# Issuing the broadcast load of the feed-forward scales ahead of the k loads in a fused attention and feed-forward kernel

## The chip, the cores and the metric

The kernel runs on one core of a Trainium2 chip. The core has TensorE (PE in the profile, with its weight loads as PEld), VectorE (DVE), ScalarE (ACT), GpSimd (POOL) and SyncE (SP), which here only issues DMAs. The metric is the device time of one launch in microseconds; lower is better. The kernel before took 1551.76 us in the median of three runs (1550.88, 1551.76 and 1554.2).

## What is computed

```python
def reference(A_x, A_wqkv, A_wo, B_x, B_w_gate, B_w_up, B_w_down):
    x = A_x                                   # 1 x 2048 x 576
    xn = _layernorm(x, axis=-1)
    s = _A_ref(xn, A_wqkv, A_wo)              # attention: 32 heads of 18, window of 256, softmax, then wo
    g = _silu(_B_ref(xn, B_w_gate, B_w_up, B_w_down))
    return x + s * g
...
    def _B_ref(x, w_gate, w_up, w_down):      # 576 -> 4608 -> 576, bilinear
        g = jnp.einsum("bsd,df->bsf", x, w_gate)
        u = jnp.einsum("bsd,df->bsf", x, w_up)
        h = g * u
        return jnp.einsum("bsf,fd->bsd", h, w_down)
```

Inputs and output are float32. The kernel multiplies in float16 with each operand split into a high and a low part, so weights are scaled by powers of two before they are split.

## The kernel before

After a head (layer norm, projection of q, k and v) the kernel runs in 72 slots. A slot does two things side by side. Its feed-forward half multiplies 512 tokens with a quarter of a group of weights: the 4608 hidden columns are cut into 18 groups of 256, numbered 0 to 17, so a group takes four slots. Its attention half, in 64 of the slots, does one pair of heads for one block of 512 queries (step `s`): scores on PE (`score_pairs`, L997), a masked maximum on DVE (`score`, L1006), the exponential and a cast to float16 on ACT (`probs` L1013, `probs_hi` L1018), the low part on POOL (`turn_probs`, L1027), a transposing DMA of both parts (L1030, tile `pt`), and the product with v on PE (`weigh`, L1039). The four query blocks of a step, i = 0 to 3, go through this chain one behind the other; the text calls their casts, low parts and transposing loads cast0 to cast3, low0 to low3 and pt0 to pt3. The tile `pp`, which casts and low parts write and the transposing loads read, has two buffers, so cast3 can start only when pt1 has been read out.

The order of the work on each engine is written out by hand. Every piece of work is put down with a slot and a time in it (`at(slot, t, f, ...)`, a slot is T = 18.65 long), the list is sorted by these times, and the instructions are issued in that order. The times say only who comes before whom; what waits for what is settled by semaphores. Every engine, SP's queue of DMAs included, goes through its own instructions in order, so that an instruction that waits holds up all that are behind it on that engine. The first 248 entries of the list are then put in another order from a table; the entries named below lie behind these.

The scales of group g are made four slots ahead. ACT squares and sums the raw weights into `am` (`ffn_amax`, L532). `ffn_spread_out` adds two halves on POOL (L536) and stores the 128 partial sums to DRAM (SP, L157, tile `sd_f`). `ffn_spread_in` reads them back, all to every partition (SP, L161, tile `spread`, 192 KB). `ffn_scale` takes the maximum over them on DVE (L544) and makes the scales by five small DVE instructions (`root_power`, L146 to L151) and three on POOL (L546 to L548).

```python
spread_in:  t = pool.tile([128, 128, n], F32, name="spread", bufs=1)
            nc.sync.dma_start(t, SD[key].partition_broadcast(128))
...
W = {..., "plo": [2.85, 5.07, 12.24, 14.56], ..., "scale": 14.98, ..., "so": 20.77, "si": 26.88, ...,
     "ld": {"k": 4.98, "q": 9.2, "v": 1.72, ...}}
at(b - 3, W["so"], ffn_spread_out, g)       # b = 4 * g
at(b - 3, W["si"], ffn_spread_in, g)
at(b - 2, W["scale"], ffn_scale, g)
```

In slot b - 2 the store then stands at 20.77 - 18.65 = 2.12 and the load at 26.88 - 18.65 = 8.23. With the times of the other DMAs of that slot, SP's queue holds in order: the store of the sums, pt0, the four loads of k for the next step (`load_k`, L968 and L969, tile `ks`), pt1, the load of the scales, the four loads of q (`load_q`, L976 and L977, tile `qs`), pt2, pt3, the load of v (L984).

PE's side of the same slot: the products of the feed-forward part are at L398, the down projection at L1133 (results in PSUM banks `dn` and `s`), and DVE adds these to the result at L1145. Banks `s` are shared: the scores of L997 lie in them until DVE's L1006 has read them, and one piece of L1133 in the slot takes over such a bank.

Of the kernel before, what the change touches and what calls it, by code (L numbers as in the profile page):

```python
# [20 lines left out]
def kernel(  # L21
# [810 lines left out]
    for half, l in ONE.items():  # L832
        for i, m in enumerate(l):
            b = R[2 * half] + 5.0 - (0 if half else 8.0 - 4.0 * i)
# [23 lines left out]
    for p in range(4):  # L858
        b = W0["qb"][p]
# [44 lines left out]
    b = R[6]  # L904
# [174 lines left out]
    def at(slot, t, f, *a):  # L1079
        todo.append((slot * T + t, len(todo), f, a))  # L1080

    first_slot = 1
    for s in range(NSTEP):
        b = first_slot + s
# [67 lines left out]
    for g in range(NG):  # L1152
        b = 4 * g
        if g > 0:
            for kind, t, u in ((1, W["ld"]["raw1"], 0.1), (2, W["ld"]["raw2"], 0.1), (0, W["ld"]["raw0"], W["raw0"] - W["ld"]["raw0"])):
                for part in range(2):
                    at(b - 3, t + u * part, ffn_raw, g, kind, part)
            for n in range(6):
                at(b - 3, W["amax"][n], ffn_amax, g, (1, 1, 2, 2, 0, 0)[n], n % 2)
            at(b - 3, W["so"], ffn_spread_out, g)  # L1160
            at(b - 3, W["si"], ffn_spread_in, g)
            at(b - 2, W["scale"], ffn_scale, g)
        for k in range(2):
            if g + k > 0:
                c = b if k else b - 2
                at(c, W["sum%d" % k][0], ffn_ratio, g, k)
                at(c, W["sum%d" % k][1], ffn_sums, g, k, 0)
                at(c, W["sum%d" % k][2], ffn_sums, g, k, 1)
                for what in range(4):
                    c = b + k if k and what == 0 else b + k - 1  # L1170
                    at(c, W["whi"][what], w_hi, g, k, what)
                    at(c, W["wlo"][what], w_lo, g, k, what)
        for k in range(2):
            for f, t in ((dn_hi, "dhi"), (dn_lo, "dlo"), (dn_low, "dlow")):
                at(max(0, b + k - 1), W[t], f, g, k)
# [174 lines left out]
    b = NSLOT - 4  # L1350
# [146 lines left out]
```

## Time and profile before

| What | Value |
|---|---|
| median of three runs | 1551.76 us (1550.88 to 1554.2) |
| the profiled execution, its own time | 1554.34 us |
| its span from first to last instruction | 1552.6 us |
| PE busy | 1532.6 us, 99% |
| DVE busy | 1293.8 us, 83% |
| ACT busy | 1047.6 us, 67% |
| POOL busy | 894.5 us, 58% |
| granted PE clock | 1.0 |

A row of a timeline holds the start in us, the duration, the engine, the line, the operation, what it writes and reads, the shape, the number of instructions merged, and in brackets how long the engine sat idle before it and what ended that. SP's rows are the issue of a DMA, not its transfer. A row of the waits holds the waiting engine and line, what it waited for, the sum in us, the number of times and the longest. PE's matmuls are pipelined and their ends are modelled, so a matmul's start is the better guide: between two slots without a stall, the same matmul comes back after 18.53 to 18.54 us.

### The profile page before, as it was taken

The numbers are of one execution on the slowest core, as the hardware profiler recorded it, in microseconds if no ns is written. First come the engines' busy times: TensorE is split into PE (matmuls) and PEld (weight loads), VectorE is DVE, ScalarE is ACT, GpSimd is POOL, SyncE is SP. The second block draws the span as 40 slices with busy tenths as digits, with TensorE's granted clock in tenths as the row PEclk, the third lists the DMA queues.
The fourth block names the chain that finished last, engine by engine and source line by source line (L and its number), as shares of the span: only waits on it lengthen the run. The fifth ranks groups of instructions, "written<-read, shape, count | busy, mean of one in ns | idle before, by whom it ended". The sixth has DMA issues, their size and how long they took to land. (4 is left out here: it accounts for less than half of the span.)

```text
span 1552.6 us, 32644 instructions
## 1 busy us (share of the span) xinstructions
PE 1532.6 (99%) x11791; PEld 882.7 (57%) x11791; DVE 1293.8 (83%) x2974; ACT 1047.6 (67%) x2038; POOL 894.5 (58%) x891
## 2 busy tenths in 40 slices
PE   8999999999999999999999999999999999999998
PEld 5554455555555555555555555555555555555576
DVE  7874777878888989898888889898989798957798
ACT  7655777676677777777777776867677777734243
POOL 5753574647465767666665757575757574822330
PEclk9999999999999999999999999999999999999999
DMA  9444556474747676776777675868685858540544
GB/s 269 132 124 166 164 103 137 92 140 86 151 93 152 137 145 140 139 137 131 151 132 146 128 156 112 163 117 158 121 163 106 167 106 168 104 103 4 113 102 152
DMA packets 562881, 206.06 MB, mean 133 GB/s; under 512 B 492320, under 2 KB 543648, under 8 KB 562720
## 3 DMA queue, kind: packets, MB, share of 16 engines
q1 hardware_dynamic: 562720, 203.98, 62.7%
q8 instruction: 92, 1.51, 0.4%
q14 instruction: 69, 0.57, 0.1%
HBM read 76.63 MB, written 23.75 MB: 65 GB/s over the span
## 5 line engine op out<-in xcount | busy, mean ns | idle before, releaser
L1133 PEld LDWEIGHTS <-hh 128*128 128x128 f16 x3456 | 328.3, 98 | 155.9 <-issue 25.5
L1133 PE MATMUL dn<-dnw,hh 128*128 128x288 f16 x1656 | 248.7, 286 | 2.1 <-DVE acc L1145 2.1
L1133 PE MATMUL s<-dnw,hh 128*128 128x288 f16 x1800 | 243.4, 286 | 3.0 <-DVE mx L1006 2.8
L1145 DVE SCALAR_TENSOR_TENSOR acc<-dn,sc,acc 128x288 f32<-128x288 f32 x260 | 133.5, 513 | 106.7 <-PE dn L1133 106.5
L398 PEld LDWEIGHTS <-wg 128*128 128x128 f16 (+1 forms) x1078 | 104.7, 97 | 121.8 <-issue 29.9
L398 PEld LDWEIGHTS <-stage 128*128 128x128 f16 x1124 | 103.8, 97 | 109.8 <-issue 12.9
L398 PE MATMUL pv<-XT,wg 128*128 128x512 f16 x616 | 154.9, 380 | 0.0
L563 POOL TENSOR_TENSOR stage<-stage 128x256 f32<-128x256 f32 (+1 forms) x180 | 146.5, 831 | 5.5
L398 PEld LDWEIGHTS <-ws 128*128 128x128 f16 x1014 | 93.4, 97 | 98.8 <-issue 13.2
L1145 DVE SCALAR_TENSOR_TENSOR acc<-s,sc,acc 128x288 f32<-128x288 f32 x284 | 139.6, 509 | 10.7 <-PE s L1133 10.1
L398 PE MATMUL up<-XT,ws 128*128 128x512 f16 (+1 forms) x532 | 139.7, 380 | 0.0
L398 PE MATMUL up<-XT,stage 128*128 128x512 f16 (+1 forms) x530 | 138.9, 380 | 0.0
L398 PEld LDWEIGHTS <-wu 128*128 128x128 f16 (+1 forms) x790 | 76.0, 97 | 95.9 <-issue 34.6
L398 PE MATMUL up<-TX,ws 128*128 128x512 f16 x456 | 111.1, 379 | 0.0
L398 PE MATMUL up<-TX,wu 128*128 128x512 f16 x450 | 109.4, 379 | 1.0 <-DVE ftb L427 1.0
L398 PE MATMUL up<-XT,wu 128*128 128x512 f16 (+1 forms) x300 | 110.1, 383 | 0.0
L398 PE MATMUL up<-TX,stage 128*128 128x512 f16 x444 | 108.2, 379 | 0.0
L398 PE MATMUL up<-XT,wg 128*128 128x512 f16 x438 | 106.5, 379 | 0.0
L1039 PEld LDWEIGHTS <-pt 128*128 128x128 f16 x2880 | 91.8, 96 | 19.5 <-issue 0.6
L1039 PE MATMUL pv<-vt,pt 128*128 128x37 f16 x2880 | 93.8, 179 | 0.4 <-DMA pt<-pp 0.4
L1011 ACT ACTIVATE mx<-mx 128x2 f32<-128x2 f32 x256 | 50.9, 199 | 47.3 <-DVE mx L1006 45.7
L532 ACT ACTIVATE spread<-stage 128x640 bf16<-128x640 f32 (+1 forms) x108 | 77.1, 714 | 1.7
(1344 smaller groups left out, 3338.7 us busy)
## 6 DMA issues: line engine op xcount, KB each, us to landing
stage<-in_B_w_down_dram SPq DMA_DIRECT2D x36, 288.0 KB
stage<-in_B_w_gate_dram SPq DMA_DIRECT2D x36, 256.0 KB
stage<-in_B_w_up_dram SPq DMA_DIRECT2D x36, 256.0 KB
vt<-v_d SPq DMA_DIRECT2D x48, 111.0 KB
ks<-qk_d SPq DMA_DIRECT2D x96, 54.0 KB
xr<-in_A_x_dram SPq DMA_DIRECT2D x16, 288.0 KB
qs<-qk_d SPq DMA_DIRECT2D x128, 36.0 KB
stage<-in_A_x_dram SPq DMA_DIRECT2D x16, 288.0 KB
```

The source lines that it names most:

```text
L398: nc.tensor.matmul(ps.rearrange("p (m n) -> p m n", n=128), w, b, start=start, stop=stop, skip_group_check=True)
L532: nc.scalar.activation(j, r, AF.Square, accum_out=SC[g, "am"][:, half, kind:kind + 1])
L563: nc.gpsimd.tensor_tensor(s_[:, d:d + 2] if d < 8 else s_[:, 8], x_, y_, op=op)
L1011: nc.scalar.activation(mx[:, 2:4], mx[:, 0:2], AF.Copy, bias=shift)
L1039: nc.tensor.matmul(PVB[s][:, j, i, :VW], pt[:, 2 * nb * j + n], VT[s][:, lo_ + n % nb, j * VW:(j + 1) * VW], start=n == 0, stop=n == 2 * n ...
L1133: nc.tensor.matmul(ps[:, :HALF], a, b, start=n == 0, stop=n == len(l) - 1)
L1145: nc.vector.scalar_tensor_tensor(d, ps[:, :HALF], SC[g][:, 9:10], d, op0=OP.mult, op1=OP.add)
```

## The change

```diff
@@ -1158,7 +1158,7 @@
             for n in range(6):
                 at(b - 3, W["amax"][n], ffn_amax, g, (1, 1, 2, 2, 0, 0)[n], n % 2)
             at(b - 3, W["so"], ffn_spread_out, g)
-            at(b - 3, W["si"], ffn_spread_in, g)
+            at(b - 3, W["si"] - (3.5 if g > 1 else 0), ffn_spread_in, g)
             at(b - 2, W["scale"], ffn_scale, g)
```

For groups 2 to 17 the load of the scales is put down at 4.73 in slot b - 2 in place of 8.23. In the sorted list nothing else changes its place. On SP's queue the load of the scales moves from behind pt1 to ahead of the four k loads and pt1: store of the sums, pt0, load of the scales, four loads of k, pt1, four loads of q, pt2, pt3. It is one DMA per group. In the slot of group 17 there are no attention steps any more, and the load passes no other DMA.

## The prediction

> **What bounds the kernel now.** I read the page first, then the waits, and then the timelines of single slots, engine by engine.
>
> ```profile
> span 1552.6 us, 32644 instructions
> ...
> PE 1532.6 (99%) x11791; PEld 882.7 (57%) x11791; DVE 1293.8 (83%) x2974; ACT 1047.6 (67%) x2038; POOL 894.5 (58%) x891
> ...
> PE s L1133 <- DVE mx L1006: 2.8, 7, 0.8
> PE s L997 <- DMA qs<-qk_d: 0.6, 2, 0.3
> ...
> DVE sc L544 <- DMA spread<-sd_f: 5.5, 6, 2.1
> ...
> 149.48 0.67 DVE L544 TENSOR_REDUCE sc<-spread 128x3 f32<-128x384 f32 x1 [2.13 <-DMA spread<-sd_f]
> ...
> ACT hh L1113 <- DVE ftd L1105: 79.3, 17, 8.6
> ```
>
> PE is the bound, so only time in which PE stands still moves the result. Its longest wait by name is that of a down projection (L1133) for a bank `s` that DVE's L1006 has yet to read; the seven I looked up lie in slots in which DVE also makes a group's scales. DVE's own wait there for the load of the scales is 5.5 us in six, of which 2.13 belong to group 0, which the change does not touch: 3.4 us in five groups. It looks as if that load were what makes DVE late. The slot of group 13, one of the five, shows otherwise.
>
> ```profile
> 1079.33 0.53 SPq L157 DMA_DIRECT2D sd_f<-am  x1
> ...
> 1082.35 0.96 SPq L968 DMA_DIRECT2D ks<-qk_d  x1
> ...
> 1086.52 1.45 SPq L1030 DMA_TRANSPOSE pt<-pp  x1
> 1088.07 0.79 SPq L161 DMA_DIRECT2D spread<-sd_f  x1
> ...
> 1090.32 0.83 ACT L1018 CAST pp<-sm__15696 128x768 f16<-128x768 f32 x1 [0.84 <-DMA pt<-pp]
> ...
> 1091.23 1.64 POOL L1027 TENSOR_TENSOR pp<-sm__15696,pp 128x768 f16<-128x768 f32 x1 [1.28 <-ACT pp L1018]
> ...
> 1091.61 0.67 DVE L544 TENSOR_REDUCE sc<-spread 128x3 f32<-128x384 f32 x1 [0.32 <-DMA spread<-sd_f]
> 1092.32 0.58 DVE L146 TENSOR_SCALAR sc<-sc 128x3 f32<-128x3 f32 x1
> 1092.93 0.17 DVE L148 TENSOR_SCALAR sc<-sc 128x3 int32<-128x3 int32 x1
> ...
> 1082.56 0.38 PE L398 MATMUL pv<-XT,wg 128*128 128x512 f16 x1
> ...
> 1093.58 0.76 PE L1039 MATMUL pv<-vt,pt 128*128 128x37 f16 x24
> ...
> 1094.90 0.28 PE L1133 MATMUL s<-dnw,hh 128*128 128x288 f16 x1 [0.56 <-DVE mx L1006]
> ...
> 1101.81 0.38 PE L398 MATMUL pv<-XT,wg 128*128 128x512 f16 x1
> ```
>
> L146 works on three elements per partition and takes 0.58 us here. It ends at 1092.90, 30 ns after POOL's low3 (1091.23 + 1.64 = 1092.87). Back from there: low3 starts 0.91 after cast3, and cast3 waited for pt1, which SP had issued 3.80 before it. Forward from there: PE gets its bank 2.00 after L146's end. So PE is held to pt1's issue + 3.80 + 0.91 + 1.64 + 0.03 + 2.00 = pt1's issue + 8.38. The load of the scales, 0.32 late, hid inside that. The control is the slot of group 8, where pt1 is early.
>
> ```profile
> 710.98 0.81 SPq L968 DMA_DIRECT2D ks<-qk_d  x1
> ...
> 712.97 1.44 SPq L1030 DMA_TRANSPOSE pt<-pp  x1
> ...
> 718.05 1.64 POOL L1027 TENSOR_TENSOR pp<-sm__10004,pp 128x768 f16<-128x768 f32 x1 [0.52 <-ACT pp L1018]
> ...
> 719.43 0.28 DVE L146 TENSOR_SCALAR sc<-sc 128x3 f32<-128x3 f32 x1
> ...
> 710.08 0.38 PE L398 MATMUL pv<-XT,wg 128*128 128x512 f16 x1
> ...
> 721.72 0.28 PE L1133 MATMUL s<-dnw,hh 128*128 128x288 f16 x1
> ...
> 728.62 0.38 PE L398 MATMUL pv<-XT,wg 128*128 128x512 f16 x1
> ...
> L146 DVE TENSOR_SCALAR sc<-sc x18: 169/225/650, 150.2 to 1390.0; 128x3 f32<-128x3 f32 x18
> ...
> 204.18 1.01 DVE L148 TENSOR_SCALAR sc<-sc 128x3 int32<-128x3 int32 x1
> ...
> 204.00 1.16 POOL L1027 TENSOR_TENSOR pp<-sm__2110,pp 128x512 f16<-128x512 f32 x1
> ```
>
> Here too L146 ends 20 ns after low3 (719.71 against 719.69), but early enough: PE starts the matmul 11.64 after the slot's first `pv` matmul without a wait, and the slot takes 18.54. In group 13 the same two numbers are 12.34 and 19.25, so the 0.70 is lost whole. Over all 18 groups L146 takes 0.17 at the least and 0.65 at the most. The last pair is an early slot, where a low part starts between two of the small instructions: L148 then takes 1.01 and ends 30 ns after it. POOL's low part and these DVE instructions do not run side by side; DVE waits for the end.
>
> **The change part by part.** Call x the time from the slot's first `pv` matmul to pt1's issue. PE's loss in a slot of scales is x + 8.38 - 11.64 = x - 3.26 where that is positive. In groups 5 to 16 (twelve slots of full width) x is 2.03, 2.94, 2.44, 2.89, 3.47, 2.94, 2.75, 2.42, 3.96, 2.33, 4.11, 4.43; the first and the last:
>
> ```profile
> 484.84 0.50 SPq L157 DMA_DIRECT2D sd_f<-am  x1
> ...
> 487.04 0.83 SPq L968 DMA_DIRECT2D ks<-qk_d  x1
> ...
> 489.06 1.33 SPq L1030 DMA_TRANSPOSE pt<-pp  x1
> ...
> 487.03 1.24 PE L398 MATMUL pv<-XT,wg 128*128 128x512 f16 x5
> ...
> 1312.36 1.43 SPq L1030 DMA_TRANSPOSE pt<-pp  x1
> ...
> 1307.93 0.38 PE L398 MATMUL pv<-XT,wg 128*128 128x512 f16 x1
> 1320.69 0.28 PE L1133 MATMUL s<-dnw,hh 128*128 128x288 f16 x1 [0.60 <-DVE mx L1006]
> ...
> L161 SPq DMA_DIRECT2D spread<-sd_f x18: 333/809/965, 145.3 to 1379.1; - x18
> ...
> 1377.03 0.34 SPq L157 DMA_DIRECT2D sd_f<-am  x1
> 1379.08 0.34 SPq L161 DMA_DIRECT2D spread<-sd_f  x1
> ```
>
> For group 16 the rule gives 1.17, and PE's matmul stands at 12.76, which is 1.12 late. Lost before, group by group: 0.21 (9), 0.70 (13), 1.12 (16), some 0.36 each in groups 7, 10, 11 and 12 where cast3 is late by itself or pt1's issue is slow, and 1.63 in group 15, where load and queries are late as well. That is 5.0 us. The waits by name bear it out: the row's 2.8 in seven, 0.14 more for each by the starts (0.56 idle in group 13 against 0.70 lost) makes 3.8, group 9 adds 0.21, and the waits for q are the rest.
>
> What the change removes: DVE's wait at L544. The load is issued where the first k load was, 5.7 us earlier in group 13 (1082.35 against 1088.07), so it lands long before DVE is there. In group 15 that is worth something; elsewhere low3 takes its place.
>
> What it adds: the load's issue, 0.81 by the median and 0.9 with the gaps around it, now stands ahead of the four k loads and pt1. The k loads have cover, as the q loads, which the same matmuls need, keep their place behind all of this. Pt1 has none. It also has 192 KB more ahead of it in the DMA queue. The queue's share I bound by 0, since pt1 is issued 2.9 after the load, and 0.7, since the load in group 13 lands 3.54 after its issue (1088.07 to 1091.61), 0.64 after that moment. I take 0.3, nearer to 0, because pt1's own issue takes 1.45, in which the queue goes on draining. So pt1 is 1.2 later, between 0.9 and 1.6.
>
> The Trainium skill, page "DMA: Bandwidth & Descriptors", section "Anatomy of one DMA", has the variable part of a transfer as its bytes by 436 GB/s, which makes 0.45 us of 192 KB; by that estimate pt1 would be 1.35 later and the sum about 1 us larger. The measured 3.54 from issue to use is longer than the 2.45 that the same section gives with its fixed 2.0.
>
> What waits for pt1: `weigh`, 3.3 us behind cast3 in group 13 (1093.58), so no loss; cast3 and ACT behind it, where the wait of 79.3 us in 17 (some 4.6 each) follows and covers it; and low3, and through it DVE and PE.
>
> The sum, with x + 1.2 and the spread no longer late. As long as low3 starts before DVE reaches L146 (9.35 after the mark, 719.43 - 710.08), that is up to x = 4.63, the loss is x - 3.26: groups 5 to 8, 10 to 12 and 14 give 0, 0.88, 0.38, 0.83, 0.88, 0.69, 0.36 and 0.27, together 4.3. In groups 9, 13 and 15 (4.67, 5.16, 5.31) low3 starts between the small instructions and the next of them waits for all of its 1.64, as at 204.18: 1.2 each after the spare time, 3.6. In group 16 (5.63) it starts about when they end: 0 or 1.2, so 0.6. After: 8.5. Groups 2 to 4 have narrow, early blocks and group 17 passes nothing: 0. The difference is 8.5 - 5.0 = 3.5 us. With 0.9 in place of 1.2 it is 2.5; with 1.6 it is 5.3.
>
> The profiled execution took 1554.34 (span 1552.6) and would take 1557.8; the median of the three runs, 1551.76, lies 2.6 below it, and I forecast that median: 1555.3.
>
> **The rivals.** Faster: the load of the scales is what holds DVE, and pt1 lands no later because the queue, not the issue, sets its landing. Then the 3.4 us of DVE's wait in five groups go, at most 3.4 for PE: 1548.4. For it speaks that the five groups are also among the losing ones; against it that L146 ends with low3 in groups 13 and 8 alike, and that a rule made from pt1's issue in group 13 gives group 16's matmul to 0.05. It decides if pt1 comes less than about 0.4 later.
>
> No difference: the shift is real but near 0.9, or lost time in one slot lets POOL and SP catch up before the next. Then it is 0 to 3 us: 1553.
>
> Slower by much more: SP, now at the load sooner, stands still until the store of the sums has landed, and k, pt1 and q all wait behind. With nothing else about, SP got to the load 2.05 after the store (group 17). The place that it moves to, the first k load's, is 3.02 after the store in group 13 and 2.20 in group 5, the closest. Were it not to land in time, q would be up to 2 us late and PE would wait at L997, as it does twice now, by about 0.8 in each of twelve groups on top: 1565. It decides where the store needs over 2.2 to 3 us.
>
> The same section of that page puts most of a DMA's fixed 2 us into the receipt from the target memory, heaviest for HBM. By that rule a load right behind its own store would stop the queue; the trace agrees with 2.05 in an idle queue and has no case in a full one.
>
> **How the numbers follow.** This kernel's measurement can tell about 0.2%, 3.1 us, from no change. The mechanism above has 0.70, split at 3.1: 0.47 slower, 0.23 the same. The faster rival has 0.12 (0.09 beyond 3.1), no difference 0.11, the store 0.07. So 0.09 faster, 0.37 the same, 0.54 slower. The likeliest case's own range is 1554.3 to 1557.1, from 2.5 and 5.3. For 8 in 10 I leave out most of the faster rival below and the store above: 1550.3 to 1559.0, which also takes in the spread of the three runs.
>
> **What would show it.** Right: DVE's wait at L544 gone in groups 9 to 16; pt1's issue some 0.9 later against the slot's mark; cast3 waiting for pt1 in nearly every slot of scales, not five; L146 or a small instruction behind it at 0.6 to 1.7 us, ending with low3; PE's wait at L1133 for L1006 grown from 2.8 us in 7 to some 6 in 10 or more. Wrong: L146 at 0.2 to 0.3 throughout and that wait near zero (the faster rival); SP waiting at L161 for `sd_f` (the store). The sum itself would be wrong if low3 falls behind the small instructions in most groups, since then it costs nothing.

## The result

The changed kernel took 1556.26 us in the median of nine executions (1555.41 to 1559.06), the kernel before 1553.29 in nine on the same chip (1550.88 to 1557.4): a ratio of 1.0021, 95% interval 1.0011 to 1.0031. A second comparison gave 1556.93 against 1553.94 and 1.0022 (1.0012 to 1.0032). It is slower by about 3.3 us.

The page of the changed kernel, and below it rows from its waits (engine, line, releaser: us, times, longest):

```profile
span 1554.0 us, 32647 instructions
...
PE 1532.3 (99%) x11791; PEld 882.5 (57%) x11791; DVE 1297.2 (83%) x2974; ACT 1047.8 (67%) x2038; POOL 893.5 (57%) x891
```
```profile
PE s L1133 <- DVE mx L1006: 3.3, 6, 1.2
...
PE s L997 <- DMA qs<-qk_d: 0.5, 1, 0.5
...
DVE sc L544 <- DMA spread<-sd_f: 2.6, 1, 2.6
...
SPq L161 <- DMA sd_f<-am: 9.6, 9, 3.5
```

DVE's wait for the load is gone from every group but group 0, which the change leaves alone: 5.5 us in six have become 2.6 in one. Yet PE's wait for its bank at L1133 has not shrunk (2.8 in seven before). The slot of group 11 shows what took the place of the load:

```profile
935.63 1.99 PE L398 MATMUL pv<-XT,wg 128*128 128x512 f16 x8
...
938.86 1.48 SPq L1030 DMA_TRANSPOSE pt<-pp  x1
...
944.27 0.83 ACT L1018 CAST pp<-sm__13419 128x768 f16<-128x768 f32 x1 [1.48 <-DMA pt<-pp]
944.28 0.67 DVE L544 TENSOR_REDUCE sc<-spread 128x3 f32<-128x384 f32 x1
944.98 0.17 DVE L146 TENSOR_SCALAR sc<-sc 128x3 f32<-128x3 f32 x1
945.18 1.64 POOL L1027 TENSOR_TENSOR pp<-sm__13419,pp 128x768 f16<-128x768 f32 x1 [1.92 <-ACT pp L1018]
945.19 1.66 DVE L148 TENSOR_SCALAR sc<-sc 128x3 int32<-128x3 int32 x1
...
948.64 0.90 PE L1133 MATMUL s<-dnw,hh 128*128 128x288 f16 x6 [1.23 <-DVE mx L1006]
```

The data are there when DVE comes to L544 (no wait in its row). Then low3, which starts 10 ns ahead of L148, holds L148 for its whole length: 1.66 us for three elements per partition. PE's matmul starts 948.64 - 935.63 = 13.01 after the slot's mark in place of 11.62, so 1.39 is lost. In groups 15 and 16, where the kernel before lost 1.66 and 1.14, the same difference is now 0.37 and 0.40. Gains and losses nearly cancel.

The same difference, start of the `s` matmul less the start of the slot's first `pv` matmul less 11.62, can be taken in each of the twelve slots of scales of groups 5 to 16. Their sum is the measure used below for what a kernel loses in these slots, in its profiled execution:

| Kernel | loss in the twelve slots, us | time against the kernel before (95% interval) |
|---|---|---|
| before | 5.26 | 1 |
| only group 17's load moved | 4.90 | 1.0002 (0.9993 to 1.0011) |
| changed: load, k, pt1, q | 4.96 and 4.82 | 1.0021 (1.0011 to 1.0031) and 1.0022 (1.0012 to 1.0032) |
| k, load, pt1, q | 8.65 | 1.0030 (1.0019 to 1.0042) |
| changed, load of 12 KB | 6.01 | 1.0014 (1.0005 to 1.0023) |
| pt1, load, k and q as before | 1.59 | 0.9979 (0.9970 to 0.9988) |
| pt1, k, load, q | 3.79 | 0.9995 (0.9987 to 1.0004) |
| k, q, pt1, load | 13.90 | 1.0089 (1.0075 to 1.0102) |
| before, low3 halved | 1.66 | 0.9987 (0.9977 to 0.9996) |
| changed, low3 halved | 0.32 | 0.9986 (0.9977 to 0.9996) |

The changed kernel's two profiled executions lose no more in these slots than the order before does.

### The profile page after: what moved, and what is told of

Its sections match the earlier page's. It is cut to its first block, busy times and chain, and to the rows that moved or that the text cites. A ratio compares the mean times of both kernels' runs of the same rounds, so it can differ in the third digit from the quotient of the medians.

```text
span 1554.0 us, 32647 instructions
## 1 busy us (share of the span) xinstructions
PE 1532.3 (99%) x11791; PEld 882.5 (57%) x11791; DVE 1297.2 (83%) x2974; ACT 1047.8 (67%) x2038; POOL 893.5 (57%) x891
## 5 line engine op out<-in xcount | busy, mean ns | idle before, releaser
L1133 PEld LDWEIGHTS <-hh 128*128 128x128 f16 x3456 | 328.3, 98 | 156.6 <-issue 26.1
L1133 PE MATMUL dn<-dnw,hh 128*128 128x288 f16 x1656 | 248.7, 286 | 2.1 <-DVE acc L1145 2.1
L1133 PE MATMUL s<-dnw,hh 128*128 128x288 f16 x1800 | 243.4, 286 | 3.6 <-DVE mx L1006 3.3
```

Of the source, the lines that this page charges most:

```text
L1133: nc.tensor.matmul(ps[:, :HALF], a, b, start=n == 0, stop=n == len(l) - 1)
```

## The experiments

The theory was that pt1's place sets low3, low3 holds DVE's small instructions, and these hold PE's bank. The rivals were the load itself, the queue (the store, k and q), and code or scatter with no mechanism in these slots.

**Nothing passed.** Only group 17's load is moved, where the slot has no other DMA to pass:

```diff
-            at(b - 3, W["si"], ffn_spread_in, g)
+            at(b - 3, W["si"] - (3.5 if g > 16 else 0), ffn_spread_in, g)
```

> The load is moved for group 17 alone, where it passes no other DMA, so every queue holds the same DMAs in the same order as before. The theory (pt1 late makes POOL's low part late, which holds up DVE's small instructions and so PE's bank) expects 0 us, and PE's wait at L1133 for L1006 at 2 to 4 us as before. The rival that the difference of the two kernels is scatter of the runs and of the head (the first moved load comes when the changed kernel's profile is already 1.15 us late) expects any value up to 3 us either way here too.

1553.44 against 1553.47. An edit of this line alone is worth nothing. The two executions of the same order also show the noise of a single slot: group 13 lost 0.72 in one and 0.47 in the other, group 9 0.22 and 0.91.

**q ahead of pt1.** This makes pt1 later and leaves the load behind pt1:

```diff
-        at(b - 1, W["ld"]["q"], load_q, s)
+        at(b - 1, 5.03 if s % 4 == 2 and s > 2 else W["ld"]["q"], load_q, s)
```

> The load of the scales stays where it was; the four q loads of the same slots are put ahead of pt1 instead, which puts pt1's issue about 1.8 us later without touching the load or its store. The theory, with pt1's issue 1.8 later in twelve slots, expects about 4 us slower (2 to 6), L146 or L148 held up to 1.2 to 1.7 us in most slots of scales. The rival that it is the load itself that harms (its 192 KB ahead of k and pt1, SP waiting for its store) expects 0 or a little faster, as q comes earlier. The rival of scatter expects 0.

1567.62, 14 us more, where 2 to 6 were expected. The direction is right and the size is not. The expectation called the load untouched; behind a later pt1 it is later too, and DVE waited for it 13.3 us in 11 groups, where it had been 5.5 in six. The wait of PE is 11.8 us in ten, and two of the ten brought a further loss, as the windows behind them show (time, sum of busy PE, PEld, DVE, ACT and POOL, then the granted clock):

```profile
800.68 1.35 PE L1133 MATMUL s<-dnw,hh 128*128 128x288 f16 x6 [1.97 <-DVE mx L1006]
801.83 2.72 PE L398 MATMUL up<-XT,wg 128*128 128x512 f16 x6
...
780.00:800.60 20.60, 18.71 (x162) 10.76 (x158) 16.04 (x41) 11.86 (x25) 9.31 (x12) 1.00 0.83 135
800.60:804.60 4.00, 3.92 (x13) 1.71 (x13) 3.09 (x11) 2.70 (x6) 3.70 (x5) 0.57 0.50 89
```

After a stall of 1.97 us the granted clock was 0.57 for the next 4 us: six matmuls of 512 columns took 2.72 us, where eight take 1.99 in the fence above. The stall of 1.95 in group 10 did the same (0.57). The two slots took 22.34 and 22.32 us in place of 18.54, of which the late matmul explains 2.1 each, so the lower clock cost some 1.7 more in each.

**k behind pt1.** Pt1 comes earlier, the load stays behind pt1 and k:

```diff
-        at(b - 1, W["ld"]["k"], load_k, s)
+        at(b - 1, 5.2 if s % 4 == 2 and s > 2 else W["ld"]["k"], load_k, s)
```

> The four k loads of the slots of scales are put behind pt1, ahead of the load, so pt1 comes 2 us earlier and the load no earlier. The theory expects low3 to be early everywhere, L146 at 0.2 to 0.65, and DVE's wait for the load (0.2 to 1.7 us in five groups), which low3 hid before, to be what is left: 0.7 us faster (2 faster to 0.5 slower). The rival that the load's late landing is all that costs expects 0.

```profile
DVE sc L544 <- DMA spread<-sd_f: 4.9, 5, 1.8
...
PE s L1133 <- DVE mx L1006: 1.5, 4, 0.8
```

1552.44, as expected. With low3 early the load is the last to come, and DVE's wait for it is bare: 4.9 us in five.

**Pt1, then the load, then k.** The same edit of k, and the load's time less 3.13 from group 2 on.

> Order pt1, load of the scales, four k loads: pt1 about 2 us earlier and the load about 2 us earlier too. The theory expects both causes of lateness gone and only the 0.36 us in some groups where cast3 is late by itself left: about 4 us faster than before (2 to 5). The rival that the load ahead of k is what costs, by its bytes or by SP's wait for the store, expects slower than before, like the changed kernel, 1 to 4 us. The rival of scatter expects 0.

```profile
PE s L1133 <- DVE mx L1006: 0.3, 2, 0.2
...
DVE sc L544 <- DMA spread<-sd_f: 2.1, 1, 2.1
```

1550.37, 3.1 us faster than the kernel before and 2.1 us faster than with k behind pt1 alone. Neither the load nor low3 is late any longer. What it says for the change: of moving the load ahead, the move past the k loads is sound, and the place ahead of pt1 is what costs.

**k, load, pt1.** The load still stands ahead of pt1, but the store has had time and k is not behind it:

```diff
-            at(b - 3, W["si"], ffn_spread_in, g)
+            at(b - 3, W["si"] - (3.2 if g > 1 else 0), ffn_spread_in, g)
```

> The load of the scales between the k loads and pt1: store, pt0, k, load, pt1, q. It still stands ahead of pt1 by its issue of some 0.6 to 0.9 us, but the store has 2 us more to land and the k loads are not behind the load. Theory (pt1 late, low3 late): like the changed kernel, 1555 to 1557. Rival (what costs is SP's wait for the store in front of the k loads, or the k loads behind it): as the kernel before or better, 1551 to 1553.5, since DVE also has its load 1.5 us sooner.

```profile
1236.26 1.99 PE L398 MATMUL pv<-XT,wg 128*128 128x512 f16 x8
...
1240.12 0.35 SPq L161 DMA_DIRECT2D spread<-sd_f  x1
1240.59 1.44 SPq L1030 DMA_TRANSPOSE pt<-pp  x1
...
1245.83 1.64 POOL L1027 TENSOR_TENSOR pp<-sm__17972,pp 128x768 f16<-128x768 f32 x1 [2.19 <-ACT pp L1018]
1245.86 1.63 DVE L148 TENSOR_SCALAR sc<-sc 128x3 int32<-128x3 int32 x1
...
1249.30 0.90 PE L1133 MATMUL s<-dnw,hh 128*128 128x288 f16 x6 [1.26 <-DVE mx L1006]
```

1558.42, above the expected 1555 to 1557. The store and k are out of the way and the loss is larger, which speaks against both as its cause. Here the cast behind pt1 started 4.3 to 4.5 us after pt1's issue in five of the six slots in which it waited, against some 3.8: a load right in front of pt1 costs it 0.5 to 0.7 in the queue, besides its issue.

**The scales made later.** Three kernels put DVE's L544 and the small instructions behind the scores' last L1006, so that low3 is no longer in their way: with the order before, with the changed order, and with pt1, load, k.

```diff
-            at(b - 2, W["scale"], ffn_scale, g)
+            at(b - 2, 17.33 if g > 1 else W["scale"], ffn_scale, g)
...
-                at(c, W["sum%d" % k][0], ffn_ratio, g, k)
-                at(c, W["sum%d" % k][1], ffn_sums, g, k, 0)
+                at(c, 21.6 if k == 0 and g > 1 else W["sum%d" % k][0], ffn_ratio, g, k)
+                at(c, 21.7 if k == 0 and g > 1 else W["sum%d" % k][1], ffn_sums, g, k, 0)
```

> The kernel before with its queue of DMAs unchanged, but from the third group on the scales are made later in their slot: DVE's maximum over the scales, its small instructions and what follows from them are put behind the scores' maximum of the last query block (L1006) and its addition, so that POOL's low3 no longer lies in their way and PE's bank no longer waits for them. Theory (low3 blocks DVE's small instructions and through them PE's bank): the 5.0 us that the kernel before loses in these slots go, of which some may come back as waits of the down projection for its scales: 1549.5, between 1548.5 and 1551.5, and PE's wait at L1133 for L1006 near zero. Rival (the load itself is what is late): the load has more time as well, so much the same gain; this run alone does not tell the two apart, the next one does. Rival (the kernel does not turn on this place at all): 1553.5.

> The changed kernel's queue (store, pt0, load, k, pt1, q) with the scales made later in their slot as in the run before. Theory: what the change costs goes through low3 and DVE's small instructions alone, so with these out of the way it costs nothing: within 1 us of the run with the old queue and late scales, 1549.5. Rival (the change costs through the queue itself: the store's wait, later k and q, PE waiting at L997): still 2 to 3 us above the run with the old queue and late scales, 1552.

> The two mends together: queue in the order store, pt0, pt1, load, k, q, and the scales made later in their slot. Theory: both mends take away the same loss, so together they give no more than the better of the two: 1549 to 1550.5, and PE's wait at L1133 for L1006 near zero. Rival (each takes away a loss of its own): the sum of both, 1546.5 to 1547.5.

They took 1563.67, 1563.53 and 1562.41, all some 9 to 10 us above the kernel before, against the expectations of 1549 to 1552. The edit moved the loss instead of taking it away. Rows of the first of the three, from the slot behind group 12's:

```profile
1045.63 1.89 DVE L175 SCALAR_TENSOR_TENSOR wu<-stage,sc,wu 128x384 f16<-128x384 f32 x1 [0.53 <-ACT wu L172]
...
1048.71 0.90 PE L1133 MATMUL s<-dnw,hh 128*128 128x288 f16 x6 [1.15 <-DVE mx L1006]
```

The weights that need the scales are split later, DVE waits for ACT there, and the bank is late one slot on. In the slots of scales themselves PE's bank no longer followed pt1: with the changed order, pt1 came 2.4 to 4.1 after the mark in groups 5 to 16, and the `s` matmul 11.62 to 11.66 after it in every one, 0.1 us lost in all twelve together. The levels of the two orders, 1.0059 (1.0046 to 1.0073) and 1.0067 (1.0054 to 1.0079), agree with a difference of nothing, but their intervals also allow 3 us. As a test of the time this is inconclusive.

**Low3 halved.** Nothing is moved; POOL's instruction gets half the columns, and ACT fills the others with a plain copy. These low parts are not the kernel's:

```diff
-        nc.gpsimd.tensor_tensor(pp[:, :, 1], sm[:, :, :n], pp[:, :, 0], op=OP.subtract)
+        h = n // 2 if i == 3 and s % 4 == 1 and s > 4 else n
+        nc.gpsimd.tensor_tensor(pp[:, :, 1, :h], sm[:, :, :h], pp[:, :, 0, :h], op=OP.subtract)
+        if h < n:
+            nc.scalar.copy(pp[:, :, 1, h:], sm[:, :, h:n])
```

> The changed kernel, with POOL's low3 in the slots of scales (from group 2 on) cut to half its columns, some 0.82 in place of 1.64 us; ACT fills the other half with a plain copy, so the low parts there are not those of the kernel. Nothing else moves. Theory (low3 blocks DVE's small instructions, and these hold PE's bank): the loss of a slot becomes x + 3.80 + 0.91 + 0.82 + 0.03 + 2.00 - 11.64 = x - 4.08. With the x of the changed kernel's trace only the slots of groups 10 and 11 still lose (0.2 and some 0.6): about 3.7 of its 5 us of loss go: 1552.5, and L146 never above 0.9 us. Rival (PE is held by the load, the store's wait or the later k and q): no effect, 1556.

> The kernel before with the same cut of low3 in the same slots. Theory: the losses that go through low3 shrink here too, but DVE's wait for the load (3.4 us in five groups of the trace) is uncovered and stays: 5.0 of loss become about 3, so 1551.5; and the kernel with the load ahead, cut in the same way, is level with it or up to 1.5 us faster, the difference turning its sign. Rival (what the change costs has nothing to do with low3): the one with the load ahead stays 3 us slower than this one, and this one is 1553.5.

The slot of group 9 with the changed order (the added lines move L1030 to L1033, L1027 to L1028 and L1133 to L1136):

```profile
784.04 1.99 PE L398 MATMUL pv<-XT,wg 128*128 128x512 f16 x8
...
787.88 1.50 SPq L1033 DMA_TRANSPOSE pt<-pp  x1
...
791.71 0.83 ACT L1018 CAST pp<-sm__11150 128x768 f16<-128x768 f32 x1 [0.76 <-DMA pt<-pp]
792.62 0.91 POOL L1028 TENSOR_TENSOR pp<-sm__11150,pp 128x384 f16<-128x384 f32 x1 [1.20 <-ACT pp L1018]
...
793.39 0.17 DVE L146 TENSOR_SCALAR sc<-sc 128x3 f32<-128x3 f32 x1
...
795.66 0.90 PE L1136 MATMUL s<-dnw,hh 128*128 128x288 f16 x6
```

Pt1 is as late as ever (3.84 after the mark), low3 starts late, and PE does not wait (11.62). The changed order took 1551.58, the order before 1551.39: the difference between them is gone (0.9986 and 0.9987). The loss in the twelve slots of the changed order fell from 4.96 and 4.82 to 0.32, nearly all of it. In the order before it fell from 5.26 to 1.66, of which 1.40 is group 15, where the load was late. So low3's length is necessary for what the change costs, though the halving also gives ACT a copy and POOL spare time, and is no test of DVE's wait by itself. The size is loose: 0.0022 and 0.0001 the other way make 3.5 us, and with four intervals of about 0.001 to each side it may be 1 to 6.

**A load of 12 KB.** The changed order, with 8 of the 128 partial sums read and the maximum taken over them 16 times; the scales are not the kernel's:

```diff
-        nc.sync.dma_start(t, SD[key].partition_broadcast(128))
+            nc.sync.dma_start(t[:, 0:8], SD[key][0:8].partition_broadcast(128))
+            return t[:, 0:8].rearrange("p a n -> p n a").unsqueeze(2).to_broadcast([128, n, 16, 8])
```

> The changed kernel with the moved load cut from 192 KB to 12 KB: it reads 8 of the 128 partial sums, and DVE's maximum goes over these 16 times, with as many elements read as before, so that the scales are not those of the reference. The place in the queue and the issue stay. This splits the load's cost to pt1 into its issue (put at 0.9) and its bytes (put at 0.3, between 0 and 0.7). Theory: most of it is the issue, so the time stays within 1 us of the changed kernel, 1555 to 1556.3, with cast3 3.8 after pt1's issue wherever it waits for it (the changed kernel's trace has 5.7 in group 5 and 5.4 in group 11). Rival (the bytes ahead of k and pt1 are the cost): 1553 or less.

1556.46 and a ratio of 1.0014: slower than before, and within the interval of the change with all its bytes. In six of seven slots in which cast3 waited, it started 3.77 to 3.84 after pt1's issue, in the other 4.82. With 192 KB it was 3.80 to 3.97 in three of five and 5.4 and 5.7 in two (first execution). So the bytes mostly cost this wait nothing. The odd late ones, 1.6 to 1.9 over the usual 3.8, are not all bytes, since one of 1.0 over it is left at 12 KB. That one and the 5.4 are both in group 11, which has a late one with the load behind pt1 as well: 4.83 with q ahead of pt1, 5.13 with the order before and the scales made later.

**The changed kernel again.** No edit; a second profiled execution.

> The changed kernel itself once more, for a second profiled execution and a narrower interval. In the first one the twelve slots of scales of groups 5 to 16 lost 4.96 us, the kernel before 5.26, so its slots do not show the 3 us that the medians differ by. Theory (low3 late costs the 3 us, and the first profile was a mild sample): 6.5 to 9 us of loss in these slots here, ratio 1.0015 to 1.0030. Rival (the 3 us come from elsewhere): again about 5 us of loss in these slots, with the difference in the head or in the end.

The theory's half of this failed. The ratio stood (1.0022), but the twelve slots lost 4.82, not 6.5 to 9. This execution lost elsewhere. Two rows of it, the windows behind them, and the same matmuls of the kernel before:

```profile
1478.02 0.90 PE L1133 MATMUL dn<-dnw,hh 128*128 128x288 f16 x6 [1.49 <-DVE acc L1145]
1479.53 1.14 PE L1133 MATMUL dn<-dnw,hh 128*128 128x288 f16 x6 [0.61 <-DVE acc L1145]
...
1472.00:1478.00 6.00, 4.53 (x29) 2.56 (x28) 5.46 (x13) 0.42 (x1) 1.42 (x2) 1.00 1.15 208
1479.80:1483.40 3.60, 3.60 (x19) 2.32 (x17) 2.15 (x4) 0.00 (x0) 0.58 (x1) 0.53 1.10 179
```
```profile
1477.08 0.90 PE L1133 MATMUL dn<-dnw,hh 128*128 128x288 f16 x6 [1.49 <-DVE acc L1145]
1478.59 0.90 PE L1133 MATMUL dn<-dnw,hh 128*128 128x288 f16 x6 [0.61 <-DVE acc L1145]
...
1478.80:1482.40 3.60, 3.60 (x32) 2.86 (x31) 2.88 (x6) 0.02 (x1) 0.63 (x1) 1.00 0.96 196
```

Behind the same two waits, long after the last slot of scales with attention, the granted clock falls to 0.53 in one execution and stays 1.00 in the other: 19 matmuls in 3.6 us against 32, and about 1.65 us. In the fourteen traces of this study, the lower clock is there at this place in four of the five with the load right behind pt0, and in one of the nine others. That looks like an effect of the change, but all executions together do not bear it out. Each has its mean granted clock on record. All five traces with a mean of 0.998 or less have a stretch at the lower clock somewhere, and one of the nine others has it. A mean of 0.998 or less stands beside 4 of 20 executions of the changed kernel and 21 of 78 of the kernel before. Without these executions the second comparison still has 1557.0 against 1553.8 on the mean.

## Why the prediction was right, and where it was not

**The time and the sign** came out: 1555.3 was forecast, 1550.3 to 1559.0 as the range, and a slowdown about as large as can be told from nothing. The account of it did not all come out, and that the forecast 3.5 us met the measured 3.3 so closely is in part luck: the term behind it was more than twice too large, and the slots in which it was to be lost do not show the loss.

**Right: the mechanism, in single slots.** DVE's wait at L544 went, and low3 took its place. L146 over the 18 groups took up to 0.65 before; in the changed kernel:

```profile
L146 DVE TENSOR_SCALAR sc<-sc x18: 169/229/1337, 151.1 to 1391.1; 128x3 f32<-128x3 f32 x18
```
```profile
L148 DVE TENSOR_SCALAR sc<-sc x18: 169/170/1655, 151.3 to 1391.3; 128x3 int32<-128x3 int32 x18
```

With low3 halved the rule gives a loss only above x = 4.08. The largest x was 3.90, and eleven of the twelve slots lost at most 0.01 us; group 8 lost 0.30, with cast3 4.53 behind pt1's issue in place of 3.80. The Trainium skill, page "SBUF — State Buffer", section "Who interferes with whom", has VectorE in its two-port modes and GpSimd share a pair of ports, taken by whoever issues first for the whole instruction while the other blocks, and counts `tensor_scalar` among the operations that can do so. The traces agree: L148 at 1.66 us beside a low3 of 1.64 that began 10 ns before it. By the same section `tensor_reduce` never contends on this chip, and L544 took 0.66 to 0.68 beside a running low part and 0.66 to 0.67 without.

**Mis-sized: the shift of pt1.** The prediction took 1.2, from 0.9 of issue and 0.3 of queue. Measured from pt0's end to pt1's issue, the median of the twelve slots went from 2.06 to 2.59 and 2.56, so the issue cost 0.5. Against the slot's mark, which is what x counts, pt1 came at 3.15 and 3.21 on the mean, where the two executions of the order before had 3.06 and 2.72. SP's rows in group 11, before and after, show why:

```profile
932.46 1.42 SPq L1030 DMA_TRANSPOSE pt<-pp  x1
933.93 0.85 SPq L968 DMA_DIRECT2D ks<-qk_d  x1
...
936.31 1.48 SPq L1030 DMA_TRANSPOSE pt<-pp  x1
937.88 0.78 SPq L161 DMA_DIRECT2D spread<-sd_f  x1
938.72 0.40 SPq L976 DMA_DIRECT2D qs<-qk_d  x1
```
```profile
934.35 1.42 SPq L1030 DMA_TRANSPOSE pt<-pp  x1
935.87 0.81 SPq L161 DMA_DIRECT2D spread<-sd_f  x1
937.07 0.33 SPq L968 DMA_DIRECT2D ks<-qk_d  x1
...
938.86 1.48 SPq L1030 DMA_TRANSPOSE pt<-pp  x1
940.38 0.81 SPq L976 DMA_DIRECT2D qs<-qk_d  x1
```

The 0.8 is not the load's price. In these rows whatever stands right behind a transposing load takes it: k and the load before, the load and q after. So the moved load brought 0.8 and took 0.5 off the first k load here (0.4 in most slots). Between k and pt1 its issue takes 0.35. The prediction added the load's 0.81 without looking at what the k load behind it would shed.

**So the sum of 8.5 against 5.0 failed.** By the prediction's own rule, with 0.5 in place of 1.2, the groups give 0.71 (9), 0.18 (6), 0.13 (8), 0.18 (10), 0 in the others that stay below x = 3.26, 1.2 in 13 and 16 and 1.35 in 15: 5.0, as much as before. If groups 7, 10, 11 and 12 keep the 0.36 that the prediction gave them for causes of their own, it is 6.2, or 1.2 more than before. The two traces have 4.96 and 4.82. In single slots the moments differ from one execution to the next (pt1's time also follows pt0's), but the sum is that: the load no longer late gives back what low3 takes. Had the shift been sized rightly, the forecast would have been the rival "no difference". Three of the prediction's own signs failed with it: pt1 was not 0.9 later against the mark, cast3 waited for pt1 in five of the twelve slots in either execution, as before, and PE's wait at L1133 for L1006 was 3.3 us in six and 2.5 in seven, not some 6 in ten or more.

**Where the 3.3 us are then.** Two profiled executions of each order have spans of 1554.0 and 1555.2 against 1552.6 and 1551.7, on the mean 2.45 apart. Of this 0.8 is the lower clock near the end, in one of the two, which the count over all executions above does not put down to the change. The mark of group 2's slot comes 0.5 later (270.31 and 269.00 against 269.16 and 269.12), before any moved load has been issued. The products of `weigh` start 0.95 later on the mean for want of their `pt`, mostly in one execution, and the `s` matmuls of L1133 over all slots 0.5. These four make 2.75, against which stands 0.3 of small differences elsewhere. The first three places are not ones that the change touches by its queue: the longer waits of `weigh` are in the slot before a slot of scales, where no moved load is in the queue. Thus it stays open how much of the 3.3 us is the mechanism, over more executions than two, and how much is in these places. That the cost needs low3's full length is shown by the halving; that the slots of scales hold the 3.3 is not.

**The store.** The prediction put its price at nothing here, with a rival of 0.07. SP did wait for it: 9.6 us in nine groups (3.5 in two before), the longest in group 2, where the load was issued 5.3 us after the store, not 2.05:

```profile
266.78 0.49 SPq L157 DMA_DIRECT2D sd_f<-am  x1
267.38 1.20 SPq L1030 DMA_TRANSPOSE pt<-pp  x1
272.12 0.34 SPq L161 DMA_DIRECT2D spread<-sd_f  x1
```

It is covered: PE's wait for q was 0.5 in one, as before (0.6 in two), and the order with k ahead of the load, which gives the store its time, was no faster. The rival was right in its first half, SP's wait, and wrong in its second, the late q.

**The bytes.** The term of 0.3 in the queue was near: 0 to 0.2 in three of the five slots above, 1.6 and 1.9 in the other two. What the bytes did lengthen is pt1's own issue: its median over the twelve slots was 1.57 and 1.62 in the changed kernel, 1.44 in both executions of the order before, and 1.44 with the load of 12 KB. The Trainium skill's 0.45 for 192 KB (page "DMA: Bandwidth & Descriptors", section "Anatomy of one DMA") lies between these too; no slot shows that value by itself. That section gives its fixed 2.0 and its 436 GB/s as a fit for DMAs issued from GpSimd, and the loads here are issued from SP, so neither the 0.45 nor the prediction's 2.45 is the page's price for them.

## What to carry to other kernels

Before a load is moved because an engine waits for it, look at what else holds that engine at the same moment: here a wait for data was hiding a wait for POOL's instruction, and moving the load traded one for the other. Ask what in the queue is the most urgent and move that first: pt1 ahead of the load and the load ahead of k took 3.1 us off, where the load ahead of pt1 took nothing off. A duration on a DMA queue can belong to the place and not to the instruction, so price an inserted issue by what stands in that place now, and count what its follower sheds.

## What the hardware showed that was not expected

- The issue of a DMA right behind a transposing load took 0.78 to 0.85 us in group 11 in either order, whichever DMA it was; the next one took 0.33 and 0.40. In the four slots of the kernel before in which pt0's own issue ran to 2.2 us or more (groups 9, 14, 15 and 16), the DMA behind it took 0.54.
- A stall of PE of 1.95 to 1.97 us was followed by some 4 us at a granted clock of 0.57. Two waits of 1.49 and 0.61, 1.5 apart, were followed by 0.53 to 0.57 in five traces of fourteen and by 1.00 in the others. The Trainium skill, page "TensorE: Matmul & The Clock Gate", part "The HAM clock gate", has a window of some 3.4 us that runs freely, after which an idle array is put to half its clock. That the same wait does and does not bring it agrees with a free-running window. The stall of 1.97 is shorter than that window, and the clock fell here all the same; narrow matmuls of 37 columns preceded it, and no run here separates the two.
- A store of 128 partial sums, a transposing load and the store's own load behind it: the last was issued 5.3 us after the store in one slot, where an idle queue had 2.05 from store to load.
